# Loading half of wd by sixteen transfers of 8 partitions in place of one of 128

## The chip, the cores and the metric

The kernel runs on one core of a Trainium2 chip. A core has a matrix engine (TensorE, PE in the profile), VectorE (DVE), ScalarE (ACT), GpSimd (POOL) and SyncE (SP), an on-chip memory of 128 partitions, accumulators that the matrix engine writes, and 16 DMA engines that move data between the on-chip memory and the chip's main memory. The metric is the device time of one execution in microseconds. Before the change it is 1001.42 us, the median of three runs between 1001.34 and 1001.9.

## The reference

One decoding step of a transformer block: four sequences, one new token each, model width 640, attention with 32 heads of 192 over a cache of 4096 keys and values, and a gated feed-forward layer of width 1536. All inputs are bf16. In outline:

```python
x = A_x                                              # [4, 1, 640]
q = (layernorm(x) @ wq) per head                     # 32 heads of 192
p = softmax(q k^T / sqrt(192)) over 4096 keys        # k_cache [4, 32, 4096, 192]
h = x + (p v, heads joined) @ wo                     # v_cache [4, 32, 4096, 192]
n = layernorm(h)
out = h + (silu(n @ w_gate) * (n @ w_up)) @ w_down   # w_down is wd, [1536, 640]
```

The two caches are by far the most of what is read: 424 MB in all, against 1.97 MB for wd.

## The kernel before

The program is one list of operations for each engine, written out in the order in which the engine is to do them (class Prog, lines 30 to 92). An operation carries the operations that it depends on; where they are on another engine, a semaphore wait is placed before it. A load adds 16 to a semaphore of its own when it has landed, and whoever uses its data waits for that.

**The stream.** Work goes through 64 steps, one for each pair of heads and sequence. Each step needs a K chunk and a V chunk of 3 MB (128 partitions of 24,576 bytes), which go into a ring of six buffers. All these loads are issued by SP, in one queue, each as soon as the ring buffer's last reader has finished (`load`, line 295). Sixteen smaller loads of wo are issued between them (`load_wo`, line 309). In each step VectorE multiplies K by the query (line 319), the matrix engine adds the products up with an identity matrix as its weights (lines 329 and 97; the weights are loaded once for twelve matmuls), and after maximum and exponential (line 365) the matrix engine multiplies V by the probabilities, two rows of V per matmul (line 391).

**The tail.** After the last step come the output projection, the second layer norm (`layer_norm`, line 251, with ln2 at line 518) and the feed-forward layer. Its weights take the place of ring buffers that have become free: wg in that of load n0, wu in that of n0 + 1, wd in that of n0 + 2, where n0 = 128 counts the K and V chunks. `behind(n)` (line 498) is the last reader of the buffer's former chunk. SP issues wg (line 501), wu (line 504), and then wd in three transfers (line 510), with a semaphore each:

```python
WDC = [(0, 6, sem("s_wd0")), (6, 10, sem("s_wd1")), (10, CF, sem("s_wd2"))]
```

wd is held as 128 partitions of CF = 12 slices of 640 numbers. Slices 0 to 5 are wd0 below, 960 KB with 7,680 contiguous bytes in each partition; slices 6 to 9 are wd1, 640 KB; slices 10 and 11 are wd2, 320 KB. The matmuls on wd (line 532) go through the slices in order, four for each slice, and each waits for guT (the gated activations, transposed on VectorE, line 528) and for the transfer that brings its slice. Then VectorE copies the result (line 535), and SP and ACT issue two output transfers of four rows each (line 536).

Of the kernel before, what the change touches and what calls it, by code (L numbers as in the profile page):

```python
# [29 lines left out]
class Prog:  # L30
# [13 lines left out]
    def dma(self, eng, fn, sem, deps=()):  # L44
        self.counts[sem] = self.counts.get(sem, 0) + 16
        t = Tok(eng, fn, [d for d in deps if d is not None], sem, self.counts[sem])
        self.ops[eng].append(t)
        return t
# [68 lines left out]
def build_kernel(nc: bass.Bass, cfg: Cfg, x, kc, vc, wq, wo, wg, wu, wd, out):  # L117
# [5 lines left out]
    CD, CF = D // 128, F // 128  # L123
# [11 lines left out]
    op, dma = pr.op, pr.dma  # L135
# [40 lines left out]
    def at(j):  # L176
        return nc.lookup_mloc(ring[j]).addr
# [3 lines left out]
    n0 = 2 * NP  # L181
    wgsb = nc.alloc_sbuf_tensor_at("wg_sb", [128, CD, F], BF16, offset=at(n0 % NS))
    wusb = nc.alloc_sbuf_tensor_at("wu_sb", [128, CD, F], BF16, offset=at((n0 + 1) % NS))
    wdsb = nc.alloc_sbuf_tensor_at("wd_sb", [128, CF, D], BF16, offset=at((n0 + 2) % NS))
# [313 lines left out]
    def behind(n):  # L498
        return lambda: released[chunks[n - NS]]
# [7 lines left out]
    WDC = [(0, 6, sem("s_wd0")), (6, 10, sem("s_wd1")), (10, CF, sem("s_wd2"))]  # L507
    wd_land = {}
    for lo, hi, k in WDC:
        t = dma("sp", lambda e, lo=lo, hi=hi: e.dma_start(  # L510
            wdsb[:, lo:hi, :], wd[:, :].rearrange("(q c) n -> q c n", c=CF)[:, lo:hi, :]), k, [behind(n0 + 2)])
        for c in range(lo, hi):
            wd_land[c] = t

# [29 lines left out]
def bass_sequential_preLN__gqa_block_cached__swiglu_ffn__decode_kernel(  # L544
    nc: bass.Bass,
    A_x: bass.AP,
    A_k_cache: bass.AP,
    A_v_cache: bass.AP,
    A_wq: bass.AP,
    A_wo: bass.AP,  # L550
    B_x: bass.AP,
    B_w_gate: bass.AP,
    B_w_up: bass.AP,
    B_w_down: bass.AP,
    out: bass.AP,
):
    B, Sq, D = A_x.shape
    assert Sq == 1
    _, H, Sk, DH = A_k_cache.shape
    assert A_wq.shape[1] == H * DH, "GQA rep must be 1 for this kernel"  # L560
    F = B_w_gate.shape[1]
    assert Sk % 128 == 0
    cfg = Cfg(B=B, H=H, NT=Sk // 128, DH=DH, D=D, F=F)
    build_kernel(nc, cfg, A_x, A_k_cache, A_v_cache, A_wq, A_wo, B_w_gate, B_w_up, B_w_down, out)
# [28 lines left out]
```

## Time and profile before

One profiled execution, in microseconds:

| what | value |
| --- | --- |
| time of the profiled execution | 1001.9 |
| its span, first to last instruction | 1000.1 |
| PE busy | 661.4 (66%) |
| DVE busy | 547.6 (55%) |
| ACT busy | 122.6 (12%) |
| read from main memory | 424.29 MB, 424 GB/s over the span |
| queue 1 (SP's loads, share of 16 engines' span) | 99.2% |
| granted clock of the matrix engine, mean | 0.831 |

Times inside the span count from its first instruction. A row of the timeline gives start, duration, engine, line, what is written and read, and, in brackets, how long the engine had been idle and what ended that. "PEld" is the loading of weights into the matrix engine. "SPq" and "ACTq" are the issuing of transfers by SP and ACT; a transfer itself runs on the DMA engines afterwards, and the time "to landing" counts from its issue to the moment at which its semaphore has its full count. A busy share of the DMA engines is a mean over the sixteen.

### The profile page before, as it was taken

Reading aid. Unit: us, or ns where it says so; the run is one execution under the profiler, and the core shown is the slowest. Engines: PE = TensorE matmul, PEld = TensorE weight load, DVE = VectorE, ACT = ScalarE, POOL = GpSimd, SP = SyncE. Lnnn points to the kernel's source line nnn. Section 1 sums busy time; section 2 is a strip of 40 time slices with the busy share of each in tenths; the row PEclk is TensorE's granted clock in tenths of the full one; section 3 lists DMA queues with packets and bytes.
Section 4 is the critical chain, followed back from the end, with each engine's and each line's share of the span. In section 5 each row is a group of like instructions: output and inputs, shape, how many; then the busy total and the mean of one; then the engine's idle time right before and its main releaser. Section 6 shows DMA issues by size and latency. Waiting matters only on the chain.

```text
span 1000.1 us, 9429 instructions
## 1 busy us (share of the span) xinstructions
PE 661.4 (66%) x4752; PEld 122.6 (12%) x3344; DVE 547.6 (55%) x450; ACT 122.6 (12%) x412; POOL 4.5 (0%) x19
## 2 busy tenths in 40 slices
PE   0676676676676676676677686676676666676686
PEld 0110110111110110110111110110110111110112
DVE  2546556546546546556546546546556546546562
ACT  0110111110110110111010110111011010110112
POOL 1000000000000000000000000000000000000000
PEclk9887887877887887887887877988888887987887
DMA  9999999999999999999999999999999999999996
GB/s 393 427 438 426 427 435 428 426 434 427 427 431 431 425 429 433 430 427 427 433 428 428 432 428 428 427 434 427 428 431 433 425 428 432 428 428 430 431 423 287
DMA packets 21849, 424.90 MB, mean 425 GB/s; under 512 B 2480, under 2 KB 2480, under 8 KB 4912
## 3 DMA queue, kind: packets, MB, share of 16 engines
q1 hardware_dynamic: 21760, 424.29, 99.2%
q8 instruction: 32, 0.52, 0.2%
q14 instruction: 9, 0.07, 0.0%
q10 hardware_dynamic: 48, 0.01, 0.0%
HBM read 424.29 MB, written 0.01 MB: 424 GB/s over the span
## 4 chain that ended last, share of the span: by engine, by line
DMA 65%; PE 23%; DVE 10%; SPq 1%; issue 1%; ACT 0%; ACTq 0%; DVEq 0%
DMA ring<-in_A_k_cache_dram 63%; PE pb L97 13%; DVE prod L319 8%; PE pb L391 3%; DMA xrow<-in_A_x_dram 2%; PE pb L329 2%; DVE sc L335 1%; PE pb L344 1%; PE pb L412 1%; PE pb L353 1%; SPq L304 1%; PE pb L286 1%; DVE msb L340 1%; PE pb L374 0%; PE pb L522 0%
## 5 line engine op out<-in xcount | busy, mean ns | idle before, releaser
L319 DVE TENSOR_TENSOR prod<-ring,qb 128x6144 f16<-128x6144 bf16 x128 | 429.1, 3353 | 303.6 <-DMA ring<-in_A_k_cache_dram 295.9
L97 PE MATMUL pb<-prod,identH 128*128 128x512 f16 x1408 | 434.2, 472 | 0.0
L344 PE MATMUL pb<-identF,msb 128*1 128x128 f32 x128 | 33.9, 362 | 301.7 <-DVE msb L340 301.7
L335 DVE TENSOR_REDUCE sc<-pb 128x32 f32<-128x512 f32 x128 | 88.1, 688 | 112.5 <-PE pb L97 112.5
L358 ACT ACTIVATE negM<-pb 128x2 f32<-128x2 f32 x64 | 11.0, 172 | 713.5 <-PE pb L353 713.5
L391 PE MATMUL pb<-ring,pbuf 128*16 128x384 bf16 x2048 | 94.7, 326 | 0.2 <-ACT pbuf L365 0.2
L365 ACT ACTIVATE pbuf<-sc,negM 64x64 bf16<-64x64 f32 x128 | 73.9, 577 | 3.0
L329 PE MATMUL pb<-prod,identH 128*128 128x512 f16 x128 | 61.3, 479 | 3.2 <-DVE prod L319 3.2
L353 PEld LDWEIGHTS pb<-negMc,ones_row 1*128 1x128 f32 x128 | 19.3, 189 | 280.5 <-issue 258.1
L391 PEld LDWEIGHTS pb<-ring,pbuf 128*16 128x16 bf16 x2048 | 46.4, 89 | 27.5 <-issue 0.5
L344 PEld LDWEIGHTS pb<-identF,msb 128*1 128x1 f32 x128 | 5.5, 81 | 329.0 <-DVE msb L340 329.0
L365 ACT ACTIVATION_READ_ACCUMULATOR pbuf<-sc,negM 64x1 f32 x128 | 41.8, 326 | 0.0
L380 ACT ACTIVATE qb<-pb 128x192 bf16<-128x192 f32 x64 | 21.2, 331 | 103.2 <-PE pb L374 103.2
L374 PEld LDWEIGHTS pb<-qsb,sel 4*64 4x64 bf16 x128 | 6.7, 101 | 163.2 <-issue 161.6
L353 PE MATMUL pb<-negMc,ones_row 1*128 1x2 f32 x128 | 24.8, 261 | 0.7 <-DVE negMc L348 0.7
L412 PE MATMUL pb<-r,orow 128*64 128x4 f32 x384 | 20.0, 231 | 0.6 <-ACT orow L399 0.6
L412 PEld LDWEIGHTS pb<-r,orow 128*64 128x64 f32 x384 | 18.6, 174 | 2.4 <-ACT orow L399 1.0
L374 PE MATMUL pb<-qsb,sel 4*64 4x192 bf16 x128 | 17.2, 265 | 1.0 <-ACT qsb L290 0.6
L348 DVE TENSOR_REDUCE negMc<-pb 1x2 f32<-1x128 f32 x64 | 17.4, 271 | 0.5 <-PE pb L344 0.5
L329 PEld LDWEIGHTS pb<-prod,identH 128*128 128x128 f16 x128 | 12.7, 99 | 32.7 <-issue 28.3
L256 PE MATMUL pb<-mv,quadm 128*128 128x2 f32 x4 | 1.2, 363 | 23.4 <-DVE mv L254 23.4
L340 DVE TENSOR_REDUCE msb<-sc 128x1 f32<-128x64 f32 x64 | 14.1, 220 | 2.2
(61 smaller groups left out, 76.1 us busy)
## 6 DMA issues: line engine op xcount, KB each, us to landing
ring<-in_A_k_cache_dram SPq DMA_DIRECT2D x64, 3072.0 KB, 29.8
ring<-in_A_v_cache_dram SPq DMA_DIRECT2D x63, 3072.0 KB, 22.8
wq_sb<-in_A_wq_dram SPq DMA_DIRECT2D x1, 7680.0 KB, 21.0
wo<-in_A_wo_dram SPq DMA_DIRECT2D x16, 480.0 KB, 23.5
ring<-in_A_v_cache_dram SPq DMA_DIRECT2D x2, 1536.0 KB, 19.3
wg_sb<-in_B_w_gate_dram SPq DMA_DIRECT2D x1, 1920.0 KB, 25.8
wu_sb<-in_B_w_up_dram SPq DMA_DIRECT2D x1, 1920.0 KB, 18.9
wd_sb<-in_B_w_down_dram SPq DMA_DIRECT2D x1, 960.0 KB, 20.8
```

Of the source, the lines that this page charges most:

```text
L97: return e.add_instruction(mybir.InstMatmult(name=e.bass.get_next_instruction_name(), engine=mybir.EngineType.PE, start_tensor_calc=start, ...
L319: tk["tt", n] = op("dve", lambda e: e.tensor_tensor(out=prod[n % NPR][:, :, :], in0=ring[slot[c]][:, h * TH:(h + 1) * TH, :], in1=qbs[i % ...
L329: tk["red", n] = op("pe", lambda e, j=j: (e.matmul if j == 0 else partial(held_matmul, e))(psR[n % 3][:, 0:TH * R], lhsT=identH[:, :], rhs ...
L335: tk["rsum", n] = op("dve", lambda e: e.tensor_reduce(sc[i % 3][:, h * TH:(h + 1) * TH], psR[n % 3][:, 0:TH * R].rearrange("q (t r) -> q t ...
L340: tk["rmax", i] = op("dve", lambda e: e.tensor_reduce(msb[i % 2][:, 0:1], sc[i % 3][:, :], AX.X, ALU.max), [g("rsum", 2 * i), g("rsum", 2 ...
L344: tk["maxT", i] = op("pe", lambda e: e.matmul(psS[0:1, 0:128], lhsT=msb[i % 2][:, 0:1], rhs=identF[:, :], start=True, stop=True), [g("rmax ...
L353: tk["maxB", i] = op("pe", lambda e: e.matmul(psS[:, 128:130], lhsT=ones_row[0:1, :], rhs=negMc[i % 2][0:1, 0:2], start=True, stop=True), ...
L365: tk["exp", i] = op("act", lambda e, hh=hh, r=r: e.activation(out=pbuf[b][r, :, 2 * b + hh], in_=sc[i % 3][r, :], func=ACTF.Exp, bias=negM ...
L374: tk["qb", i] = op("pe", lambda e, hh=hh: e.matmul(psQ[64 * hh:64 * hh + 64, 0:DH], lhsT=sel[32 * n:32 * n + B, b, :], rhs=qsb[32 * n:32 * ...
L380: tk["qbc", i] = op("act", lambda e: e.activation(out=qbs[i % 2][:, :], in_=psQ[:, 0:DH], func=ACTF.Copy, scale=QS), [g("qb", i), g("tt", ...
L391: tk["pv", i] = op("pe", lambda e, t=t, n=n: e.matmul(psO[p % 2][32 * n:32 * n + 4 * B, 0:2 * DH], lhsT=pbuf[b][:, t:t + 2, :].rearrange(" ...
L412: tk["oT", p] = op("pe", lambda e, j=j, hh=hh, k=k: e.matmul(psO[p % 2][64 * hh:64 * hh + 64, OC + B * j:OC + B * (j + 1)], lhsT=orow[p % ...
```

## The change

The first of wd's three transfers, slices 0 to 5 on 128 partitions, is issued as sixteen transfers of 8 partitions each, one after the other, all on SP's queue and on the same semaphore. The matmuls on these slices wait for the sixteenth's count, 256 in place of 16. The change's description says that these transfers run on DMA engines 0 to 7. The second and third transfer, and everything that computes, are as they were.

```diff
     for lo, hi, k in WDC:
-        t = dma("sp", lambda e, lo=lo, hi=hi: e.dma_start(
-            wdsb[:, lo:hi, :], wd[:, :].rearrange("(q c) n -> q c n", c=CF)[:, lo:hi, :]), k, [behind(n0 + 2)])
+
+        nr = 8 if lo == 0 else 128
+        for r in range(0, 128, nr):
+            t = dma("sp", lambda e, lo=lo, hi=hi, r=r, nr=nr: e.dma_start(
+                wdsb[r:r + nr, lo:hi, :], wd[:, :].rearrange("(q c) n -> q c n", c=CF)[r:r + nr, lo:hi, :]),
+                k, [behind(n0 + 2)])
         for c in range(lo, hi):
             wd_land[c] = t
```

## The prediction

> **What bounds the kernel now.** I read the page's chain of work first, then the timeline of the last 30 us, then the DMA issues and landings there, then busy time by the microsecond.
>
> ```profile
> DMA 65%; PE 23%; DVE 10%; SPq 1%; issue 1%; ACT 0%; ACTq 0%; DVEq 0%
> DMA ring<-in_A_k_cache_dram 63%; PE pb L97 13%; DVE prod L319 8%; PE pb L391 3%; DMA xrow<-in_A_x_dram 2%; PE pb L329 2%; DVE sc L335 1%; PE pb L344 1%; PE pb L412 1%; PE pb L353 1%; SPq L304 1%; PE pb L286 1%; DVE msb L340 1%; PE pb L374 0%; PE pb L522 0%
> ```
>
> The chain is the streaming of K (and of V, which shares its queue): the kernel reads 424 MB at 425 GB/s. The name wd_sb is not in it. The change begins long after the last K chunk is in, so what counts is the tail, here in the timeline (start, duration, engine, line; the bracket is idle time before it and what ended it):
>
> ```profile
> 958.54 3.36 DVE L319 TENSOR_TENSOR prod<-ring,qb 128x6144 f16<-128x6144 bf16 x1 [4.83 <-DMA ring<-in_A_k_cache_dram]
> ...
> 972.02 0.33 SPq L504 DMA_DIRECT2D wu_sb<-in_B_w_up_dram  x1
> ...
> 972.39 1.38 SPq L510 DMA_DIRECT2D wd_sb<-in_B_w_down_dram  x3
> ...
> 994.92 0.85 DVE L528 STREAM_TRANSPOSE guT<-gu 128x384 bf16<-128x384 bf16 x1
> 995.82 1.43 PEld L532 LDWEIGHTS pb<-wd_sb,guT 128*4 128x4 bf16 x48 [2.33 <-DVE guT L528]
> 995.82 1.77 PE L532 MATMUL pb<-wd_sb,guT 128*4 128x160 bf16 x48 [1.62 <-DVE guT L528]
> 997.64 0.33 DVE L535 CAST outsb<-pb 128x160 bf16<-128x160 f32 x1 [1.88 <-PE pb L532]
> 998.00 0.67 SPq L536 DMA_DIRECT2D out_dram<-outsb  x2
> ```
>
> From 958.5 us on, no wait names a DMA; the 48 matmuls on wd start when guT is ready, at 995.82. When wd lands is seen in the issues from 930 us on (KB each, median us from issue to landing):
>
> ```profile
> wu_sb<-in_B_w_up_dram SPq DMA_DIRECT2D x1, 1920.0 KB, 18.9
> wd_sb<-in_B_w_down_dram SPq DMA_DIRECT2D x1, 960.0 KB, 20.8
> wd_sb<-in_B_w_down_dram SPq DMA_DIRECT2D x1, 640.0 KB, 21.9
> ...
> wd_sb<-in_B_w_down_dram SPq DMA_DIRECT2D x1, 320.0 KB, 22.2
> ```
>
> Three issues of 0.43 us in 1.38 us start 0.475 us apart: 972.39, 972.86, 973.34. So wd0 (slices 0 to 5) lands at 993.2, wd1 (6 to 9) at 994.8, wd2 (10, 11) at 995.5, and wu at 972.02 + 18.9 = 990.9. The matmuls use the slices in order: the last of 48 starts 0.34 us (its duration in the tile's view) before 997.59, so they start (997.25 - 995.82)/47 = 0.030 us apart; wd1 is needed at 995.82 + 24 x 0.030 = 996.55, wd2 at 997.04. Slack: wd0 2.6 us, wd1 1.8, wd2 1.5. That slack is the cover under which everything below lies or does not.
>
> Busy time by the microsecond (last two columns: mean busy share of the 16 DMA engines, GB/s):
>
> ```profile
> 987.00:988.00 1.00, 0.40 (x12) 0.06 (x4) 0.94 (x4) 0.00 (x0) 0.00 (x0) 0.50 1.05 428
> ...
> 990.00:991.00 1.00, 0.17 (x4) 0.10 (x8) 0.74 (x2) 1.00 (x1) 0.00 (x0) 0.50 0.56 233
> ...
> 992.00:993.00 1.00, 1.00 (x16) 0.42 (x12) 0.00 (x0) 0.34 (x1) 0.00 (x0) 0.50 0.56 230
> ...
> 994.00:995.00 1.00, 0.20 (x4) 0.00 (x0) 0.64 (x2) 0.00 (x0) 0.00 (x0) 0.50 0.36 143
> 995.00:996.00 1.00, 0.18 (x8) 0.18 (x12) 0.77 (x1) 0.00 (x0) 0.00 (x0) 0.50 0.01 3
> ```
>
> From 990 to 993 us, 0.56 of the 16 engines work: nine. Seven have finished, since each engine has its own queue and they have drifted apart. The trace's landing marks, one for each engine's share of a transfer, say how far: wd0's sixteen lie at 986.5 to 987.2 (five engines), 987.9, 989.5, 991.2 and 991.3, and seven at 992.9 to 993.2. A transfer has landed when its slowest engine has.
>
> **The change part by part.** wd0's one transfer of 128 partitions becomes sixteen of 8; wd1 and wd2 stay. No compute instruction is added, removed or moved on PE, DVE, ACT or POOL.
>
> *Issues on SP.* Fifteen more, at 0.475 us from start to start (the row above): 15 x 0.475 = 7.1 us. The last of the sixteen starts at 979.5, wd1's at 980.0, wd2's at 980.5. Behind them SP has only the output of 998.0. The earliest engine is through with wu at 984.2 (wu's first landing mark), so the queues hold wd before they come to it, by 3.7 us; cost 0. From below nothing can be gained by it. From above: the longest single SP issue in the trace took 1.6 us (the K load at 119.9); sixteen of these put wd1's issue at 998.0, and the end about 5 us later.
>
> *Which engines.* The four-row transfers of the trace show the split:
>
> ```profile
> q1 hardware_dynamic: 21760, 424.29, 99.2%
> ...
> q10 hardware_dynamic: 48, 0.01, 0.0%
> ```
>
> Queue 10 carries six four-row transfers (four of x, two of the output): 48/6 = 8 packets each, four rows and four completion marks. The 151 transfers of 128 partitions make 144 packets each (128 rows, 16 marks), and with two outputs this is 151 x 144 + 16 = 21760, as the row says. So four rows ran on four engines, and eight should run on eight. [...]
>
> *Bytes.* Eight engines now carry 122,880 B of wd0 each in place of 61,440, the other eight none. The rate of one engine: wd1 is 40,960 B for each and lands 994.8 - 993.2 = 1.56 us after wd0, 26 GB/s; so 61,440 B are 2.34 us. Engines 0 to 7 come 2.34 us later to wd1 and wd2, engines 8 to 15 come 2.34 us earlier. What this does to the landings depends on which group holds the nine late engines. Only seven are early, so eight engines hold at least one of the nine.
> - Lower end: the late one among 0 to 7 is one of the two at 991.2. wd0 then lands at 991.3 + 2.34 = 993.6, wd1 at 995.2, wd2 at 996.0, all before need: 0. A gain is excluded, because no instruction waits for wd now.
> - Upper end: one of the seven last is among 0 to 7. wd0 lands at 993.2 + 2.34 = 995.5, still before 995.82; wd1 at 997.1, against 996.55; wd2 at 997.9, against 997.04.
>
> I take the upper end: the lower one needs all seven last engines to sit in 8 to 15, and nothing that I can show says so.
>
> *Sixteen endings in place of one.* After a transfer's last row an engine does a completion mark of 0.009 us and starts the next transfer 0.006 us later, although the landing is counted 0.4 us after the mark (packet records at every boundary of large transfers). So fifteen more cost 15 x 0.015 = 0.2 us. No row shows large transfers of one row for each engine back to back. Nearest are the outputs: two on SP, issued at 998.00 and 998.39, whose rows start at 998.78 and 999.21, 0.43 us apart for issues 0.39 apart, so little is added by the first's ending. Upper end: each transfer waits for the one before, for an output's 1.1 us from issue to landing: 16 x 1.1 = 17.6 us from 990.9, wd0 at 1008.5, wd2 at 1010.8, 14 us too late. I take 0.2, from the boundaries, which are the same queue and the same moment.
>
> [...]
>
> *Sum.* wd2 lands at 995.5 + 2.34 + 0.2 = 998.05 and its matmuls start 1.0 us later than 997.04. DVE's copy, queued behind them, the output and the end follow by the same amount. wd1's own lateness (0.75 us) lies within that. The profiled execution took 1001.9 us (span 1000.1 and 1.8 around it) and was the slowest of three, 0.5 us above the median, 1001.42. On the median: 1001.42 + 0.9 = 1002.3, taking 0.9 as the slowest of 0 to 7 need not be the slowest of all.
>
> **The rivals.**
> - *Hidden (0).* The seven last engines lie in 8 to 15; every part of wd lands before its need. For it: the 1.5 us of slack, and the drift has a regular cause that may pick a half: 16 KB instruction packets (queue 8, 32 on the page) each hold one engine up for about 1.5 us. Against it: nothing ties them to 8 to 15. Time 1001.4.
> - *Slower, by a cost for each small transfer on the engine.* Its place is the queue of the late engine among 0 to 7 between 990 and 995 us. It decides (over 2 us) from 2.0 - 0.8 = 1.2 us over 15 endings, 0.08 us each; at a third of a landing (0.37 us) it is 0.8 + 15 x 0.37 = 6.4 us, time 1007.8; at a whole one 1015. For it: 60 KB transfers back to back are not in this trace. Against it: the boundaries at 0.015 us.
> - *Slower, by SP's issues.* wd2 must be issued by about 993.5 (an output's 1.1 us and two shares of data, 2.3 us, before 997), 17 issue steps after 972.39, which is 1.2 us for each; at the 1.6 us above the end comes at 1006. Against it: the usual 0.33 to 0.43 us.
> - *Faster.* Engines 8 to 15 lose 2.34 us, and the end of the loads comes earlier. For it: the nine engines at work alone up to 993. Against it: no wait in the tail ends with a load. Time 1001.4 again; over 0.2% only by something that the profile does not show.
> - *Not what it says:* eight rows spread over all sixteen engines. Then loads are as before: 1001.4 plus the endings, hidden.
>
> **How the numbers follow.** Delayed by up to 1 us: 0.45. Hidden, or spread evenly: 0.33. A cost for each transfer of over 0.08 us: 0.14. Issues: 0.04. Faster: 0.04. A measurement of this kernel can tell about 0.2%, 2 us, from no change, so the first two are both "same": 0.78; slower 0.18, faster 0.04. The likeliest is 1002.3. The range begins under the hidden case by the spread of the runs (0.6 us) and a little, at 1000.7, and reaches into the cost for each transfer up to 0.15 us (0.8 + 2.3 = 3.1 us), 1004.5; what is left out is most of the two slower cases and the faster one.
>
> **What the profile after would show.** Queue 1 with 21760 - 144 + 16 x 16 = 21872 packets, if eight engines were used; eighteen issues on wd_sb about 0.475 us apart, ending near 981; the landing of wd1 and wd2, and whether PE's first wd matmul or a later one waits for a DMA; the last matmul's end against 997.6. The prediction is wrong if wd lands after 999, if SP still issues at 990, or if the main loop before 958 us has moved by more than a microsecond, which nothing in the change explains.

## The result and the profile after

The changed kernel takes 1006.42 us, the median of four runs (1006.26 to 1006.79); beside it the kernel before took 1001.66 (four runs, 1001.34 to 1002.74). The ratio is 1.0046 with a 95% interval of 1.0029 to 1.0064: 4.8 us slower. The forecast was 1002.3 us, too small a change to be told from none, with a range up to 1004.5. It was wrong, and by a mechanism, not by a rounding.

The chain of work on the page of the changed kernel now has wd in it:

```profile
DMA 67%; PE 21%; DVE 10%; SPq 1%; issue 0%; ACTq 0%; ACT 0%
DMA ring<-in_A_k_cache_dram 63%; PE pb L97 13%; DVE prod L319 7%; PE pb L391 3%; DMA wd_sb<-in_B_w_down_dram 2%; DMA xrow<-in_A_x_dram 2%; PE pb L329 2%; DVE sc L335 1%; PE pb L344 1%; SPq L304 1%; PE pb L353 1%; PE pb L412 1%; PE pb L286 1%; DVE msb L340 1%; SPq L513 0%
```

The timeline of the tail shows where (lines are four further on than before):

```profile
972.69 6.30 SPq L513 DMA_DIRECT2D wd_sb<-in_B_w_down_dram  x18
...
990.73 0.35 DVE L266 STREAM_TRANSPOSE lnT<-lnrow 128x160 bf16<-128x160 bf16 x1
...
991.13 1.77 PE L526 MATMUL pb<-wg_sb,lnT 128*4 128x384 bf16 x20 [1.90 <-DVE lnT L266]
...
994.40 1.77 PE L526 MATMUL pb<-wu_sb,lnT 128*4 128x384 bf16 x20 [1.50 <-DMA wu_sb<-in_B_w_up_dram]
...
996.89 0.85 DVE L532 STREAM_TRANSPOSE guT<-gu 128x384 bf16<-128x384 bf16 x1
...
999.39 0.97 PE L536 MATMUL pb<-wd_sb,guT 128*4 128x160 bf16 x24 [3.21 <-DMA wd_sb<-in_B_w_down_dram]
1000.79 1.22 PE L536 MATMUL pb<-wd_sb,guT 128*4 128x160 bf16 x24 [0.43 <-DMA wd_sb<-in_B_w_down_dram]
1001.57 0.10 PEld L536 LDWEIGHTS pb<-wd_sb,guT 128*4 128x4 bf16 x8 [0.42 <-DMA wd_sb<-in_B_w_down_dram]
1002.06 0.33 DVE L539 CAST outsb<-pb 128x160 bf16<-128x160 f32 x1 [4.33 <-PE pb L536]
```

In the kernel before, these two rows stood in the same place:

```profile
990.42 0.35 DVE L266 STREAM_TRANSPOSE lnT<-lnrow 128x160 bf16<-128x160 bf16 x1
...
992.39 1.82 PE L522 MATMUL pb<-wu_sb,lnT 128*4 128x384 bf16 x20
```

Four waits for a DMA now stand in the tail, where there was none: for wu, wd0, wd1 and wd2. The first of them is for wu, a load that the change does not touch and that stands ahead of wd in the queue. The profiled executions can be added up between the same two points: the copy at line 535 began at 997.64, here (line 539) at 1002.06, 4.42 us later. Of this 0.31 was there before the feed-forward layer began (lnT's transpose at 990.42 and 990.73). guT's transpose began 1.97 later, so 1.66 came with the wait for wu. The first wd matmul began 3.57 later, so 1.60 came with wd0. The 25th matmul, the first on wd1, began at 996.57 before and at 1000.79 here, 4.21 later, so 0.64 came with wd1. The last 0.21 came with wd2: the eight matmuls on it began at 1001.57, after its last mark at 1001.53. 0.31 + 1.66 + 1.60 + 0.64 + 0.21 = 4.42.

Issues and landings of the tail (KB each, us to landing; the profile gives no landing for the sixteen):

```profile
wu_sb<-in_B_w_up_dram SPq DMA_DIRECT2D x1, 1920.0 KB, 22.0
wd_sb<-in_B_w_down_dram SPq DMA_DIRECT2D x16, 60.0 KB
wd_sb<-in_B_w_down_dram SPq DMA_DIRECT2D x1, 640.0 KB, 22.6
...
wd_sb<-in_B_w_down_dram SPq DMA_DIRECT2D x1, 320.0 KB, 23.0
```

wu lands 22.0 us after its issue in place of 18.9: 994.4 by its last mark, in place of 990.9. SP was done with all eighteen issues at 979.0. So wu's lateness comes neither from the issues nor from the longer queue, which stands behind it. Something slowed the engines while they carried wu. The busy time from 986 to 990 us shows it (last two columns: busy share of the DMA engines, GB/s), for the kernel before:

```profile
986.00:990.00 4.00, 1.73 (x28) 1.21 (x26) 2.10 (x10) 0.56 (x2) 0.00 (x0) 0.55 0.89 366
```

and after:

```profile
986.00:990.00 4.00, 1.83 (x34) 1.44 (x32) 1.89 (x8) 0.28 (x1) 0.00 (x0) 0.70 0.88 239
```

The engines are busy for the same share, 0.89 and 0.88, and move 366 and 239 GB/s. They do not wait between transfers; each packet takes longer. The trace's packet records say the same: a row of wd0 (7,680 bytes) took 0.29 us before and 0.40 after, in the median; a row of wu (15,360 bytes) 0.575 before and 0.86 after, of those begun when wd0's first had begun. The slowing is common to all: of the rows begun between 987 and 989 us, those of wd0, wu and wd2 took 0.434, 0.885 and 0.146 us in the median, and 0.293, 0.574 and 0.102 in the kernel before, 1.4 to 1.5 times as long each.

### The profile page after: what moved, and what is told of

Its sections match the earlier page's. It is cut to its first block, busy times and chain, and to the rows that moved or that the text cites. A ratio compares the mean times of both kernels' runs of the same rounds, so it can differ in the third digit from the quotient of the medians.

```text
span 1004.5 us, 9444 instructions
## 1 busy us (share of the span) xinstructions
PE 658.7 (66%) x4752; PEld 121.5 (12%) x3344; DVE 547.6 (55%) x450; ACT 122.6 (12%) x412; POOL 4.5 (0%) x19
## 3 DMA queue, kind: packets, MB, share of 16 engines
q1 hardware_dynamic: 21872, 424.29, 99.2%
## 4 chain that ended last, share of the span: by engine, by line
DMA 67%; PE 21%; DVE 10%; SPq 1%; issue 0%; ACTq 0%; ACT 0%
DMA ring<-in_A_k_cache_dram 63%; PE pb L97 13%; DVE prod L319 7%; PE pb L391 3%; DMA wd_sb<-in_B_w_down_dram 2%; DMA xrow<-in_A_x_dram 2%; PE pb L329 2%; DVE sc L335 1%; PE pb L344 1%; SPq L304 1%; PE pb L353 1%; PE pb L412 1%; PE pb L286 1%; DVE msb L340 1%; SPq L513 0%
```

## The experiments

Eleven of the twelve runs change how wd0 is loaded (one of them, with partitions 0 to 63 written twice, also the matmuls that read it). Each row of the table is one kernel, timed against the kernel before on the same chip. "wd0 row" and "wu row" are the medians of the packet records as above, in us; "twice" is the share of wd0's 128 rows that took over 1.7 times the fastest.

| wd0 loaded as | ratio to before (95%) | wd0 row | wu row | twice |
| --- | --- | --- | --- | --- |
| one of 128 (before) | 1 | 0.291 | 0.575 | 0 of 128 |
| 16 of 8 neighbours (the change) | 1.0046 (1.0029 to 1.0064) | 0.398 | 0.860 | 11 |
| 16 of 8, step 16 | 1.0069 (1.0054 to 1.0084) | 0.494 | 1.050 | 64 |
| 16 of 8 neighbours, rows of wd in step 16 | 1.0043 (1.0028 to 1.0058) | 0.405 | 0.861 | 4 |
| 16 of 8 in step 16, neighbouring rows of wd | 1.0065 (1.0050 to 1.0080) | 0.508 | 1.030 | 67 |
| 8 of 16 neighbours | 1.0028 (1.0017 to 1.0039) | 0.420 | 0.808 | 25 |
| 8 of 16, step 8 | 1.0032 (1.0019 to 1.0044) | 0.493 | 0.901 | 63 |
| the change, 16 semaphores | 1.0042 (1.0027 to 1.0057) | 0.406 | 0.887 | 9 |
| 6 of 128, one slice each | 0.9998 (0.9989 to 1.0007) | none of this size | 0.575 | none |
| 2 of 64 neighbours | 1.0039 (1.0024 to 1.0054) | 0.522 | 0.914 | 68 |
| 16 of 8, step 4 | 1.0047 (1.0032 to 1.0062) | 0.361 | 0.587 | 47 |
| 16 of 8, step 4, partitions 0 to 63 twice | 1.0009 (0.9999 to 1.0019) | 0.291 | 0.573 | 0 |
| 8 of 16, step 4 | 1.0030 (1.0020 to 1.0040) | 0.398 | 0.802 | 49 |

### Neighbouring partitions, neighbouring rows, or many small transfers

The edit with step 16 for both, against the kernel before (`ps` are the partitions written, `rs` the rows of wd read). The next two have `slice(8 * r, 8 * r + 8)` in place of one of the two, and the fourth has eight transfers with `slice(16 * r, 16 * r + 16)` for both:

```diff
-        t = dma("sp", lambda e, lo=lo, hi=hi: e.dma_start(
-            wdsb[:, lo:hi, :], wd[:, :].rearrange("(q c) n -> q c n", c=CF)[:, lo:hi, :]), k, [behind(n0 + 2)])
+
+        for r in range(16 if lo == 0 else 1):
+            ps, rs = (slice(r, 128, 16), slice(r, 128, 16)) if lo == 0 else (slice(0, 128), slice(0, 128))
+            t = dma("sp", lambda e, lo=lo, hi=hi, ps=ps, rs=rs: e.dma_start(
+                wdsb[ps, lo:hi, :], wd[:, :].rearrange("(q c) n -> q c n", c=CF)[rs, lo:hi, :]),
+                k, [behind(n0 + 2)])
```

> Sixteen transfers of 8 partitions as in the changed kernel, but each takes every 16th partition (r, r+16, ...) and the rows of wd that belong to them, in place of 8 neighbours. Same number of transfers, of completion marks, of engines (8) and of bytes for each. Theory P (engines that write into the same 8 neighbouring partitions at one time slow one another and all that write there) and theory H (engines that read 8 neighbouring rows of wd at one time do) both expect packets of 7,680 bytes back at 0.29 us and those of wu at 0.58, wu landed near 991, and only the longer queue of eight engines left: about 1 us over the kernel before, 1002.4. Theory T (it is the many small transfers or their marks) expects the packets at 0.4 to 0.5 us as in the changed kernel and 1006.4.

> As the changed kernel, 8 neighbouring partitions for each transfer, but the rows of wd read are every 16th, so the rows of slices 0 to 5 come to the wrong partitions and the output is not the reference's; bytes and shapes are the same. P: slow as the changed kernel, 7,680-byte packets at 0.4 to 0.5 us, 1006.4. H: back to 1002.4. T: 1006.4.

> The other half of that pair: every 16th partition written, 8 neighbouring rows of wd read, so again slices 0 to 5 lie at the wrong partitions and the output is not the reference's. P: 1002.4 and packets at 0.29 us. H: 1006.4 and packets at 0.4 to 0.5. T: 1006.4.

> wd0 in eight transfers of 16 neighbouring partitions. Each engine has one row of each, so all sixteen carry the same bytes as in the kernel before and no queue is longer; there are 128 engine marks, as many as in the changed kernel. If the longer queue of eight engines were all (the prediction's own step), 1001.4. P and H: engines that are in step still meet in 16 neighbouring partitions or rows, so packets of wd0 and wu are stretched, though over two groups of 8 and for 2.3 us of each engine's time in place of 4.7: 1002 to 1005. T: half of the transfers, the same number of marks: 1004 to 1006.

Measured: +0.69% (6.3 us at the medians) with step 16 in both, +0.43% with the rows of wd alone, +0.65% with the partitions alone, and +0.28% for eight transfers of 16. Both P and H fell, since spreading the partitions made it worse, not better. One half of the pair says more than was asked: which rows of main memory are read makes no difference (0.398 and 0.405 us; 0.494 and 0.508), and which partitions are written does. In step 16, half of wd0's rows took about twice the usual time or more, as if two engines had shared something. T was left standing, but T had no reason to depend on the partitions. A longer queue for eight engines could not be all of it either: in the run with 16 neighbours each of the eight transfers has 16 marks (queue 1 has 21760 - 144 + 8 x 32 = 21872 packets), so that no engine has more bytes than before, and it was 0.28% slower.

### Whose partitions, whose semaphore, how many marks

Eight transfers of 16 partitions in step 8 (`ps` and `rs` as above):

```diff
+        for r in range(8 if lo == 0 else 1):
+            ps, rs = (slice(r, 128, 8), slice(r, 128, 8)) if lo == 0 else (slice(0, 128), slice(0, 128))
```

The changed kernel with a semaphore for each transfer (the matmuls wait for all of them):

```diff
-                k, [behind(n0 + 2)])
+                k or sem(f"s_wd0_{r}"), [behind(n0 + 2)]))
...
-                start=False, stop=(c == CF - 1), skip_group_check=True), [gut, wd_land[c], ln2])
+                start=False, stop=(c == CF - 1), skip_group_check=True), [gut, ln2] + wd_land[c])
```

Six transfers of one slice each, in place of the one:

```diff
+        nc_ = 1 if lo == 0 else hi - lo
+        for c0 in range(lo, hi, nc_):
+            t = dma("sp", lambda e, c0=c0, c1=c0 + nc_: e.dma_start(
+                wdsb[:, c0:c1, :], wd[:, :].rearrange("(q c) n -> q c n", c=CF)[:, c0:c1, :]),
+                k, [behind(n0 + 2)])
```

Two halves, against the changed kernel:

```diff
-        nr = 8 if lo == 0 else 128
+        nr = 64 if lo == 0 else 128
```

> wd0 in eight transfers of 16 partitions as in the run with 16 neighbours, but every eighth partition (r, r+8, ...). [...] Same transfers, marks, rows and bytes. [...] Theory N (transfers of one row for each engine, or their 128 marks, are what costs): packets at 0.4 to 0.5 us and +2.7 us as with 16 neighbours.

> The changed kernel, but each of the sixteen transfers has a semaphore of its own, and the matmuls wait for all sixteen. Theory M (marks that arrive on one semaphore from many engines hold one another up): packets back at 0.29 and 0.58 us, about +1 us over the kernel before. [...]

> wd0 in six transfers of 128 partitions, one slice (1,280 bytes in each partition) each. [...] If marks or the number of transfers in a short time cost (N in that form, and M): wu's packets at 0.8 us or more, +2 us or more. [...]

> [...] Only 32 marks, four rows each, no engine with more bytes than before. [...] N and M: two transfers in place of one cost nothing, packets at 0.29 and 0.58, 0 us.

Measured: +0.32%, +0.42%, -0.02% (no difference), +0.39%. M fell: sixteen semaphores change nothing. N and T fell on two sides: six transfers with 96 marks cost nothing, and two transfers with 32 marks cost nearly as much as the change. The waits of the run with two halves:

```profile
PE pb L534 <- DMA wd_sb<-in_B_w_down_dram: 3.6, 2, 3.4
...
PE pb L524 <- DMA wu_sb<-in_B_w_up_dram: 0.8, 1, 0.8
```

So it is neither the smallness nor the number. What the harmless forms have in common is 128 partitions. Neighbours are not what costs either: with 16 partitions in step 8, which reach over all 128, 63 of wd0's 128 rows took about twice the time. No view here names the partitions of an engine.

### Every fourth partition

Neighbours, step 8 and step 16 were all slow. The next three runs write every fourth partition: by eight engines, by eight engines with partitions 0 to 63 alone, and by sixteen.

Sixteen transfers of 8 partitions in step 4:

```diff
+        for m in range(16 if lo == 0 else 1):
+            s0 = 32 * (m // 4) + m % 4
+            ps, dst = slice(s0, s0 + 29, 4) if lo == 0 else slice(0, 128), wdsb
```

The same with partitions 0 to 63 twice, in place of 64 to 127:

```diff
+            if lo == 0 and m >= 8:
+                ps, dst = slice(s0 - 64, s0 - 35, 4), wdspare
...
+        h = 64 if c < 6 else 128
...
-                psH[32 * n:32 * n + B, 0:DQ], lhsT=guT[:, c, 0:B], rhs=wdsb[:, c, n * DQ:(n + 1) * DQ],
+                psH[32 * n:32 * n + B, 0:DQ], lhsT=guT[0:h, c, 0:B], rhs=wdsb[0:h, c, n * DQ:(n + 1) * DQ],
```

Eight transfers of 16 partitions in step 4:

```diff
-        for m in range(16 if lo == 0 else 1):
-            s0 = 32 * (m // 4) + m % 4
-            ps, dst = slice(s0, s0 + 29, 4) if lo == 0 else slice(0, 128), wdsb
+        for m in range(8 if lo == 0 else 1):
+            s0 = 64 * (m // 4) + m % 4
+            ps, dst = slice(s0, s0 + 61, 4) if lo == 0 else slice(0, 128), wdsb
```

> Sixteen transfers of 8 partitions on eight engines as in the changed kernel, but each takes every fourth partition (s, s+4, ... s+28). [...] Theory N (transfers of one row for each engine cost by themselves): packets at 0.4 to 0.5 throughout and +4 to +5 us.

> As the run with every fourth partition, but the last eight transfers write partitions 0 to 63 again, into spare space, in place of 64 to 127, and the matmuls on slices 0 to 5 leave out partitions 64 to 127: this part of the sum is missing from the output. [...] N: +4 to +5 us.

> [...] No engine has more bytes than in the kernel before. [...]

The run with partitions 0 to 63 twice shows whether sixteen transfers of 8 cost by themselves. Its output lacks a part of the sum, but it has the same sixteen transfers of 8, same marks, same bytes on as many engines (queue 1 has 21872 packets again), and its ratio is 1.0009 (0.9999 to 1.0019): they do not. Every one of its 128 wd0 rows took 0.291 to 0.298 us. Its window and its matmuls on wd:

```profile
986.00:990.00 4.00, 2.01 (x42) 1.62 (x38) 1.51 (x6) 0.49 (x1) 0.00 (x0) 0.88 0.95 389
```

```profile
wu_sb<-in_B_w_up_dram SPq DMA_DIRECT2D x1, 1920.0 KB, 17.6
```

```profile
991.79 0.35 DVE L268 STREAM_TRANSPOSE lnT<-lnrow 128x160 bf16<-128x160 bf16 x1
...
996.28 0.85 DVE L535 STREAM_TRANSPOSE guT<-gu 128x384 bf16<-128x384 bf16 x1
...
997.18 1.10 PE L540 MATMUL pb<-wd_sb,guT 64*4 64x160 bf16 x48 [1.61 <-DVE guT L535]
998.34 0.32 DVE L543 CAST outsb<-pb 128x160 bf16<-128x160 f32 x1 [1.21 <-PE pb L540]
```

389 GB/s against 239, wu landed in time, and the matmuls wait for guT again. The run with step 4 over all partitions shows the two cases within one kernel. Its windows, while the early engines are at the first eight transfers (partitions 0 to 63) and then at the last eight (64 to 127):

```profile
984.00:986.00 2.00, 1.41 (x28) 0.65 (x20) 0.18 (x1) 1.32 (x3) 0.00 (x0) 1.00 0.89 361
987.00:989.00 2.00, 0.60 (x18) 0.30 (x16) 1.51 (x6) 0.00 (x0) 0.00 (x0) 0.79 0.99 208
```

From 984 to 986 us the rows of wd0 take 0.291 us and those of wu 0.573. From 987 to 989 they take 0.576 and 1.14: half speed. That these engines write partitions 64 to 127 is not by itself what costs: the last four rows of wd0 in this run, begun from 997.5 us on, when the other engines had little left, took 0.29 to 0.30 us.

Whom the slowing reaches is another matter. From 992.9 to 993.5 us it is a pair at a time: one row of wd0 took 0.58 us and beside it two of wd1, one after the other, 0.40 each, while the other rows of wd0, wd1 and wd2 took their usual 0.29, 0.20 and 0.10, which would fit two engines that share something and get half each; no view shows what it is. But at 988.0 us five engines were at wd0, eight at wu and two at wd1, and all fifteen rows took twice their time. In pairs, five engines can meet at most five others, so at least five engines were at half speed beside none of the five. How the slowing spreads, no run here shows. The cost of this run, +0.47% (4.8 us), is not wd0's delay alone: wu landed 21.1 us after its issue in place of 18.9. Sixteen partitions in step 4 cost +0.30%, so it is not the step.

### The same in the stream

```diff
+        elif c == ("K", 32):
+            for a in (0, 64):
+                landed[c] = [dma("sp", lambda e, a=a: e.dma_start(
+                    r[a:a + 64, :, :].rearrange("q t d -> q (t d)"), src(c)[a:a + 64]), S_ring[slot[c]], deps)]
```

> The kernel before, with wd loaded as there, but one K chunk in the middle of the stream (K of step 32, 3 MB) comes in two transfers of 64 neighbouring partitions in place of one of 128. Same bytes for each engine, one transfer and 16 marks more. [...] N and a price for each small transfer or mark: no change that can be told.

Measured: a ratio of 1.0107 (1.0090 to 1.0124), 10.8 us at the medians, for one 3 MB chunk of 128. Windows of 10 us of that run, with the engines' busy share and GB/s at the end, first here and then in the kernel before:

```profile
500.00:510.00 10.00, 7.59 (x59) 1.20 (x37) 2.70 (x3) 1.66 (x6) 0.00 (x0) 0.93 1.04 231
510.00:520.00 10.00, 0.00 (x0) 0.00 (x0) 0.00 (x0) 0.00 (x0) 0.00 (x0) 0.58 0.94 229
```

```profile
500.00:510.00 10.00, 7.71 (x59) 1.20 (x37) 3.77 (x4) 1.66 (x6) 0.00 (x0) 0.91 1.00 430
510.00:520.00 10.00, 6.90 (x20) 0.58 (x6) 7.16 (x6) 0.70 (x3) 0.00 (x0) 0.66 1.01 431
```

A row of 24,576 bytes took 1.78 us in the median of those begun from 500 to 516 us, and 0.915 in the kernel before. Twenty microseconds at 230 GB/s carry what takes 20 x 230/430 = 10.7 in the kernel before, so 9.3 us are lost here, and PE and DVE have no busy time at all in the second window. N, and a price for each small transfer or mark, expected no change and fell here too. More was slowed than the chunk's own 3.1 MB: the twenty microseconds carried 4.6 MB.

## Why the prediction was wrong

*The issues on SP (0 us):* right. They took 0.35 us each, less than the 0.475 taken, and ended at 979.0.

*Which engines:* right as to their number. Queue 1 has 21872 packets, as forecast for eight engines; that they are 0 to 7, no run shows, since no view names an engine. That one of the seven last engines is among those with wd0 was right too, as far as the landing marks tell, which do not name their engines: in the run with partitions 0 to 63 twice the seven last ended wu at 990.5 to 991.0; five marks of wd1 follow at 992.2 to 992.5, which is wd1 alone behind wu, and two as late as 996.8 and 997.1, which is wd0 and wd1.

*Bytes (2.34 us later on eight engines):* the arithmetic was right and the premise was not. The step that failed is the sentence "the rate of one engine ... 26 GB/s; so 61,440 B are 2.34 us". It took the rate to be the engine's own. The runs show that it depends on the partitions that are written at one time: a row of wd0 took 0.291 us in the median in the kernel before, where the loads of the stream and of the tail's weights each write 128 partitions, and 0.361 to 0.522 in the ten kernels of the table that are slow, which write a part of them. So no row of these loads in the kernel before could show otherwise. In the changed kernel a row took 0.398 us, 19 GB/s, in the median, and wd0 landed at 999.25 by its last mark in place of the 995.7 that the sum had. In the run with partitions 0 to 63 twice, where every row of wd0 took 0.291 to 0.298 us, the latest engine ends wd1 6.1 us after the latest end of wu (997.1 and 991.0); the sum's terms give 4.68 + 0.2 + 1.56 = 6.4. wd2 landed there at 997.92, against the sum's 998.05. That the same run's time is +0.9 us (interval -0.1 to +1.9), the forecast's number, is luck as far as its trace shows: no matmul waits for wd in it. lnT's transpose began 1.37 us later than in the kernel before, ahead of anything that wd could do, and the 48 matmuls then took 1.10 us in place of 1.77, so the copy at the end began 0.70 us later.

*Sixteen endings in place of one (0.2 us):* right for the endings. In the run with partitions 0 to 63 twice the rows stand at 0.291 us with all their marks. The rival "a cost for each small transfer on the engine" gave up to 14 us and a place, the queue of the late engine, and a part of that range holds the result; but its mechanism is wrong. Two transfers of 64 partitions have almost none of its cost and are as slow.

*What wu does:* missing altogether. The prediction asked only when wd is late. It gave no term to a load ahead of wd in the same queue. But engines drift up to 6.7 us apart here (wu's marks in the kernel before, 984.2 to 990.9), so early engines were at wd0 while late ones were at wu, and the late ones' rows of wu took 0.860 us in place of 0.575. With wd0 written to other partitions, 0 to 63 twice, they took 0.573, so it is the early ones' writes that slowed them. Of the 4.42 us, 1.66 came in by wu. The slack of 1.5 us that I gave as the cover was for wd alone; wu's own slack (990.9 against 992.39) was as small.

*The profile's signs:* "wd lands after 999" was named as a sign of a wrong prediction; wd2 landed at 1001.5.

What is shown and what is argued: that it is the set of partitions written, and not rows, semaphores, marks, number of transfers or bytes, is shown by the runs. That two engines share something and get half each is an estimate, from the 47 to 68 of wd0's 128 rows that took about twice the time in six runs, from the change of speed within one run (0.291 to 0.576 us), and from the pairs at 993 us in it; no view names the partition or the engine of a row. How the slowing reaches the others, and so the size of 4.8 us, stays open. In the changed kernel itself halves do not give the figures: the longest row of wd0 took 0.567 us and the median 0.398, while wu's rows took 1.5 times as long all the same; no run shows why.

## What to carry to other kernels

A load is not described by its bytes and its queue. The partitions that it writes at one time bear on how long its rows take, and a load over a part of the partitions can slow whatever the other engines are carrying, loads ahead of it included: wu's rows took 0.860 us in place of 0.575. Of the forms here that write a part of the partitions in each transfer, only every fourth one of partitions 0 to 63, by eight engines, did not (0.291 and 0.573). Cut a load along the free dimension, keeping all 128 partitions (six such pieces cost nothing here, a ratio of 0.9998), and not along the partitions (two halves cost 0.39%, and 10.8 us for a single chunk in the stream). When a profile shows the DMA engines busy at an unchanged share and fewer GB/s (0.88 and 239 here, against 0.89 and 366), look at the packets' durations by size before looking for gaps.

## What the runs showed of the hardware that was not expected

- How long a row takes depends on the partitions that are written at one time: a row of wd0 took 0.291 us in the median with 128 partitions to a transfer and 0.494 with 8 in step 16. The slowing is not confined to that load's own rows: in step 4 at 988 us all fifteen rows in flight, of wd0, wu and wd1, took twice their time (from 987 to 989 us 0.576 for wd0 and 1.14 for wu).
- The DMA engines drift apart by whole microseconds within one queue: in the kernel before, the sixteen shares of wd0 landed from 986.5 to 993.2. A likely cause is the 16 KB instruction packets (queue 8): three engines' marks for wg stood at 984.3 to 984.5 and six later, but of wu only two at 988.9 to 989.0 and seven later, so that one engine fell about 1.55 us behind its neighbours, and the one such packet of that stretch ran at 986.3 us and took 1.07.
- The time that SP needs to issue a transfer depends on its partitions: 0.34 us from start to start for 8 neighbours, 0.46 for 16, 0.61 for 8 in step 16, 0.67 for 8 in step 4. With six transfers of 128 partitions and short rows, the sixth issue and those of wd1 and wd2 took 3.2 to 4.0 us each in place of 0.43, while much was queued. Neither cost anything that can be told here: the run with partitions 0 to 63 twice, in step 4, has a ratio of 1.0009 (0.9999 to 1.0019), and the six transfers 0.9998.
